# Matmuls of constants in TensorE's early gaps, and new planner constants, in a fused attention and MLP kernel

## The chip, the cores and the metric

The kernel runs on one core of one Trainium2 chip. A core has five engines with a queue each: TensorE (PE; its weight loads are shown apart as PEld), ScalarE (ACT), VectorE (DVE), GpSimd (POOL) and SyncE (SP), which here only issues DMAs. Each queue runs in its own order, and the engines wait for one another through semaphores. The metric is the device time of one execution in microseconds (us); the figure for a kernel is the median of several runs.

## The reference: what is computed

Inputs are q, k and v of shape (8, 8, 576, 64): eight batches, eight heads, 576 positions, 64 values. For each head two attentions are computed and added. In short, with `factor = 4`:

```python
q_d, k_d, v_d = (means over groups of 4 positions)      # 144 positions
out_d = softmax(scale * q_d @ k_d.T) @ v_d              # dense, small
out_up = repeat(out_d, 4)
mask = abs(i - j) < 4
out_local = softmax(where(mask, scale * q @ k.T, -1e9)) @ v
x = out_up + out_local                                  # to (4608, 512)
h = x @ w_in                                            # 512 -> 2048
out = (h * sigmoid(h)) @ w_out                          # 2048 -> 512
```

The output has 4608 rows of 512 float32. So there are 64 heads of attention, and behind them an MLP over 4608 tokens. The 512 values of a token come from all eight heads of its batch, so a token can enter the MLP only when all heads of its batch are done.

## The kernel before, in words

**The work.** Heads are handled in pairs (32) and in quads of two pairs (16); a batch is four pairs, or two quads. For each quad the tasks are, by their names in the code:

- `lqk`, `lv` (L403 on): SP loads q, k and v of a pair into staging tiles. For the first pairs some staging lies in tiles that are used only later (`gT`). `cq`, `ck`, `cw`: casts to bf16 on ACT, POOL or DVE.
- `TQ`, `TK` (`ph_T`): nine 128x128 transposes on PE into PSUM; `oq`, `ok` copy them out on ACT or DVE; `mq`, `mk` sum groups of four, on DVE or, for the first quads, on POOL.
- `S1`, `S2`: scores of the local band and of the small dense attention, followed by exponentials `e1`, `e2`, `e3` on ACT and `k`, the multiplication with the band's mask on DVE.
- `ZD` or `Z`: 56 small matmuls that sum the exponentials. For the first four quads ("direct") DVE forms a reciprocal split over three bf16 parts (`zs`, five operations) and PE spreads it over partitions (`RB`). For later quads DVE writes the reciprocal, SP sends it to memory (`scr`) and reads it back spread out (`Rb`).
- `VD`: 30 matmuls that downsample v for the direct quads; `cv` copies the result to `vd` in two operations. It needs the casts of both pairs' v.
- `PV`: probabilities times v of both attentions for a pair; `pa`, `pb` multiply with the reciprocals on DVE into `xo`; `ad` (L774) adds the two attentions on POOL and writes `xT`, the MLP's input.

The MLP takes 512 tokens at a time, nine such tiles. `g1` (L785 on) is four matmuls for one of 16 blocks of 128 hidden values, then a tanh on ACT (`th`) and a gate on DVE (`st`) into `gT`. `g2` is four matmuls of a quarter of one 128-token output block; behind the fourth quarter the result is copied to `osb` and stored. A `g1` of tile 0 needs the adds of the first four pairs (`ad0` to `ad3`).

**The order.** Nothing of the order is written out by hand. Before anything is emitted, a planner in the kernel (class `Prog`, and the loop at the kernel's end) plays the program through with a cost for each operation. At every step it takes, among the tasks that could start, one by its earliest start and by a priority: the dictionary `TUNE` holds one number for each kind of task, added to the start time. `seq` in `TUNE` is the order in which loads become ready for planning; `w0` to `w3` are the four quarters of `w_in`, `w4` to `w7` those of `w_out`, issued by POOL. The outcome is a fixed list for each engine, with semaphore waits. When the chip is late on one instruction, the rest of its engine's list waits behind it.

**PSUM.** There are eight banks: two `duo` pairs for attention, and `hps` and `ops`, which also serve attention until the first `g1` is planned. `best_bank` names a free bank.

The costs that the planner takes for PE are multiplied by 1.3 for what starts before 40 us of its own clock (L173).

Of the kernel before, what the change touches and what calls it, by code (L numbers as in the profile page):

```python
# [17 lines left out]


TUNE = {  # L20
    "tol": 0, "mode": -232, "lead": 52, "rep": 445, "g1": 743, "g2": 955, "TQ": -753, "TK": -555, "VD": -4771,
    "S1": -1491, "S2": -116, "ZD": -14158, "Z": 48, "RB": 750, "PV": -3123, "cw": 7042, "cv": 1981, "cq": -1820,
    "ck": 15017, "mask": -18259, "neg": 1254, "dm": 3746, "ones": 936, "Tq": 4085, "Tk": -7783, "mq": 1194,
    "mk": -571, "e1": -363, "e2": -2893, "e3": -162, "k": -4513, "rc": -10797, "zs": -8518, "rb": -4806,
    "pa": 6979, "pb": 21288, "th": 325, "st": -3659, "ob": 1342, "oq": 5641, "ok": 6128, "ad": 3736,
    "lqk": 14883, "lv": 9202, "lvq": 9231, "r": 13022, "b": 10108, "tq": -1796, "tk": 9538, "out": -3589,
    "age": 768, "alt": 538, "late": 900, "slack": 500, "slack1": 300, "direct": 4, "dma": 9, "cx": 6286,
    "c.dm": 29564, "c.pad": -7887, "c.vd": -1605, "band": 11289, "sel": 7263,
    "seq": ["lqk0", "lv0", "lqk1", "lqk2", "lv1", "lqk3", "lv2", "lv3", "w1", "lqk4", "w2", "w0", "w3", "lqk5",
            "lv4", "lqk8", "lqk7", "lqk6", "lv5", "w6", "w7", "lv6", "w4", "lqk9", "lv7", "w5"],  # L30
}


# [19 lines left out]
class Prog:  # L53
# [80 lines left out]
    def op(self, eng, fn, r=(), w=(), dma=None, cost=0, issue=450, tau=90, lock=False):  # L134
        op = Op(eng, fn)
        op.cost = cost
        op.pos = len(self.streams[eng])
        know = self.know[eng]
        deps = []
        for x in r:  # L140
            if x.psum:
                deps += [(o, False) for e, o in x.last.items() if e != eng]
            else:
                deps += [(o, True) for o in x.writers]
        for x in w:
            if x.psum:
                deps += [(o, False) for e, o in x.last.items() if e != eng]
            else:
                rd = x.readers + ([op] if x in r else [])
                if rd:  # L150
                    x.prev, x.readers, x.writers = rd + x.writers, [], []
                deps += [(o, dma is not None or eng != "PE") for o in x.prev]
                if dma is not None:
                    deps += [(o, True) for o in x.writers if o.dsem != dma]
        if eng == "POOL" and cost >= 400 and not dma and self.streams["POOL"] and not self.streams["POOL"][-1].dsem:

            deps.append((self.streams["POOL"][-1], True))
        deps = [(d, f) for d, f in deps if d is not op]
        t = self.free[eng]
        for d, f in deps:  # L160
            if d.eng != eng or d.dsem:
                t = max(t, d.end + self.LATENCY[d.eng])
        if dma:
            op.t0 = t
            t += issue if eng == "SP" else 650 if eng == "ACT" else 800
            self.free[eng] = max(t, self._dma(op, eng, t, cost, tau) if eng != "POOL" else t)
            if eng == "POOL":
                self._dma(op, eng, t, cost, tau)
        else:
            if lock or eng == "POOL":  # L170
                t = max(t, self.lock)
            op.t0 = t
            self.free[eng] = op.end = t + cost * (1.3 if eng == "PE" and t < 40000 else 1)  # L173
        if lock or (eng == "POOL" and not dma):
            self.lock = op.end
        op.deps = [d for d, f in deps]
        op.tag = self.tag
        deps.sort(key=lambda df: -(df[0].pos if not df[0].dsem else 1 << 30))
        for d, f in deps:
            self._dep(op, d, know, f)  # L180
        op.waits = [
            w for w in op.waits
            if not any(v is not w and v[2].K.get(w[0], -1) >= w[1] for v in op.waits)
        ]
        for x in r:
            if x.psum:
                x.last[eng] = op
            elif x not in w:
                x.readers.append(op)
        for x in w:  # L190
            if x.psum:
                x.last[eng] = op
            else:
                x.writers.append(op)
        op.K = dict(know)
        if dma:
            self.dcount[dma] = self.dcount.get(dma, 0) + 16
            op.dsem, op.dval = dma, self.dcount[dma]
            op.K[dma] = op.dval
        else:  # L200
            op.K[eng] = op.pos
        self.streams[eng].append(op)
        return op
# [36 lines left out]
def bass_hourglass_attn__then__act_silu_kernel(  # L240
# [9 lines left out]
    with kctx:  # L250
        E = kctx.enter_context
        P = Prog()
        res = {}

        def R(name, psum=False):
            if name not in res:
                res[name] = Res(name, psum)
            return res[name]

        def sb(name, shape, dt, n=1):  # L260
            ts = [E(nc.sbuf_tensor(f"{name}{i}", shape, dt)) for i in range(n)]
            return ts if n > 1 else ts[0]
# [6 lines left out]
        th = sb("th", [128, 512], F32, 2)  # L269
# [27 lines left out]
        id_bf = sb("id_bf", [128, 128], BF16)  # L297
        mask_bf = sb("mask_bf", [128, S_], BF16)
        onesZ = sb("onesZ", [128, 12, 32], BF16)
        neg = sb("neg", [128, 2], F32)  # L300
        band = sb("band", [128, 2, 10, 2], BF16)
        sel = gT[1][:, 11:16, :].rearrange("p a (y m) -> p (a y) m", m=128)
# [3 lines left out]
        duo = [E(nc.psum_tensor(f"duo{i}", [128, 2, 512], F32)) for i in range(2)]  # L306
# [3 lines left out]
        duo_r = [[R(f"{n}{x}", True) for x in y] for n, y in (("duo0", "ab"), ("duo1", "ab"), ("h", "01"), ("o", "01"))]  # L310

        direct, by_dma = tuple(range(TUNE["direct"])), tuple(range(TUNE["dma"], NQUAD))
# [105 lines left out]
        def order_T(s, x, eng):  # L418
            y, h = s % NQT, s % 2
            src = (qr if x == "q" else kr)[:, :, 64 * h:64 * h + 64].rearrange("p r g -> p g r")  # L420
            dst = (qT if x == "q" else kT)[y][:, :].rearrange("p (g r) -> p g r", r=9)
            r, w = [R(f"{x}r")], [R(f"{x}T{y}")]
            if eng == "DVE":
                P.op("DVE", lambda e: e.tensor_reduce(dst, src.unsqueeze(3), mybir.AxisListType.X, ALU.add),
                     r=r, w=w, cost=1165)
            else:
                copy(eng, dst, src, r, w, {"ACT": 1220})
# [43 lines left out]
        ng1, ng2 = [0], [0]  # L471
# [3 lines left out]
        def is_free(banks):  # L475
            return not any(pend.get(b.name) for b in banks)
# [14 lines left out]
        def best_bank():  # L491

            bs = [(d, x) for d in range(4 if ng1[0] == 0 else 2) for x in range(2) if is_free([duo_r[d][x]])]
            return min(bs, key=lambda b: (is_free([duo_r[b[0]][1 - b[1]]]), P.ready("PE", [], [duo_r[b[0]][b[1]]]), used[b[0]]),
                       default=None)
# [13 lines left out]
        done = set()  # L509
# [25 lines left out]
        mode = ["full"]  # L535
# [318 lines left out]
        seq = TUNE["seq"]  # L854
# [22 lines left out]
        for i in range(NQUAD):  # L877
# [10 lines left out]
            for s in (2 * i, 2 * i + 1):  # L888
                y, m, j = s % NQT, s % NP_, s % 2
                for x in "qk":  # L890
                    if i in by_dma:
                        task(("DVE", "ACT") if x == "q" else ("ACT", "DVE"), f"o{x}{s}",
                             [f"t{x}{i}", nm("S2", s - NQT), nm("mq", s - NQT), nm("mk", s - NQT)],
                             lambda e, s=s, x=x: order_T(s, x, e), [R(f"{x}r")], [R(f"{x}T{y}")])
# [78 lines left out]
        def choose(eng):  # L973

            c = [(s, t) for t in Q[eng][:LOOK[eng]] for s in [start(eng, t)] if s is not None]
            if eng != "PE":
# [10 lines left out]
                c.append((s + TUNE[k] + (TUNE["lead"] * lead * (1 if k == "g1" else -1)) + (TUNE["rep"] if last[0] == k else 0), s, k))  # L987
            return min(c, key=lambda x: x[0])[1:] if c else None

        LOOK = {"PE": 60, "ACT": 60, "DVE": 300, "POOL": 300, "SP": 70}  # L990
        last, log = [""], []
        const_id()
        while True:
            best = [(c[0], e, c[1]) for e in P.ENGS for c in [choose(e)] if c]
            if not best:
                break
            s, eng, t = min(best, key=lambda x: x[0])
            if isinstance(t, str):
                P.tag = last[0] = t
                n = ng1 if t == "g1" else ng2  # L1000
                (g1 if t == "g1" else g2)(*divmod(n[0], 16))
                log.append((s, t))
                continue
            for e in t[8]:
                Q[e] = [x for x in Q[e] if x is not t]
            if t[0] == f"ad{oldest[0]}":
                oldest[0] += 1
            for b in t[7]:
                pend[b.name] -= 1
            P.tag = t[0]  # L1010
            if eng == "PE":
                last[0] = t[0]
            t[2](eng)
            done.add(t[0])
            log.append((s, t[0]))
# [36 lines left out]
```

## Time and profile before

| | |
|---|---|
| median of 7 runs | 373.25 us (370.89 to 374.38) |
| profiled execution, its time | 373.78 us |
| profiled execution, its span from first to last instruction | 372.1 us |
| mean granted TensorE clock | 0.976 |
| PE busy | 346.1 us, 93% |
| DVE, ACT, POOL busy | 232.9, 218.3, 163.3 us |
| MLP matmuls, `g1` | 576, of which 544 into `hps`, 437 ns each |
| MLP matmuls, `g2` | 576, 381 ns each |
| moved by DMA | 66.13 MB, mean 178 GB/s |

The page cuts the span into 40 slices of 9.3 us. A digit of 9 is an engine busy for nine tenths of a slice or more; PEclk is the clock granted to TensorE in tenths of full speed. Matmul durations overlap, so 437 ns is not the spacing: four `g1` matmuls follow one another in 0.93 us at full clock. In a timeline, a bracket behind a line tells how long the engine was idle before it and what ended that. Time in which PE is idle, or slow, counts here; time in which another engine idles counts only through PE.

### The profile page before, as it was taken

Reading aid. Unit: us, or ns where it says so; the run is one execution under the profiler, and the core shown is the slowest. Engines: PE = TensorE matmul, PEld = TensorE weight load, DVE = VectorE, ACT = ScalarE, POOL = GpSimd, SP = SyncE. Lnnn points to the kernel's source line nnn. Section 1 sums busy time; section 2 is a strip of 40 time slices with the busy share of each in tenths; the row PEclk is TensorE's granted clock in tenths of the full one; section 3 lists DMA queues with packets and bytes.
Section 4 is the critical chain, followed back from the end, with each engine's and each line's share of the span. In section 5 each row is a group of like instructions: output and inputs, shape, how many; then the busy total and the mean of one; then the engine's idle time right before and its main releaser. Section 6 shows DMA issues by size and latency. Waiting matters only on the chain.

```text
span 372.1 us, 8434 instructions
## 1 busy us (share of the span) xinstructions
PE 346.1 (93%) x3498; PEld 213.5 (57%) x3498; DVE 232.9 (63%) x375; ACT 218.3 (59%) x362; POOL 163.3 (44%) x203
## 2 busy tenths in 40 slices
PE   1676899999979989999999999999999999999996
PEld 0565567566646655566556555556566555555542
DVE  4777478778578946795598469967765333333310
ACT  4967476587537753886588647766743343443321
POOL 7937665787288529643782286066113000000000
PEclk9978599999999999999999999999999999999999
DMA  7999979969999999999997899784144010001012
GB/s 235 322 359 345 185 218 261 193 184 254 245 241 256 189 284 242 242 237 258 249 243 182 187 190 174 201 179 101 35 116 106 28 56 28 30 28 56 30 56 85
DMA packets 85095, 66.13 MB, mean 178 GB/s; under 512 B 62785, under 2 KB 64833, under 8 KB 85057
## 3 DMA queue, kind: packets, MB, share of 16 engines
q1 hardware_dynamic: 80832, 59.31, 65.9%
q0 software_dynamic: 4224, 6.29, 7.3%
q8 instruction: 27, 0.44, 0.5%
q14 instruction: 12, 0.09, 0.1%
HBM read 53.67 MB, written 9.88 MB: 171 GB/s over the span
## 4 chain that ended last, share of the span: by engine, by line
PE 82%; DMA 7%; POOL 3%; DVE 3%; ACT 2%; SPq 1%; issue 1%; POOLq 0%; ACTq 0%
PE ops L541 35%; PE hps L541 34%; PE duo L541 11%; DMA scr<-rr 3%; DMA Rb<-scr 3%; PE duo L551 2%; POOL xT L774 2%; DMA qs<-in_q_dram 1%; POOL qb L382 1%; DVE xo L754 1%; DVE Pt L611 1%; ACT Pt L588 0%; SPq L443 0%; POOL w_out_bf L834 0%; DVE xo L757 0%
## 5 line engine op out<-in xcount | busy, mean ns | idle before, releaser
L541 PE MATMUL hps<-xT,w_in_sb 128*128 128x512 f32 x544 | 171.1, 437 | 4.5 <-DVE gT L797 2.9
L541 PE MATMUL ops<-w_out_bf,gT 128*128 128x512 bf16 x576 | 145.5, 381 | 0.0
L797 DVE SCALAR_TENSOR_TENSOR gT<-th,hps 128x512 bf16<-128x512 f32 x136 | 92.6, 683 | 81.1 <-ACT th L795 80.5
L795 ACT ACTIVATE th<-hps 128x512 f32<-128x512 f32 x136 | 81.5, 600 | 96.7 <-PE hps L541 96.0
L541 PEld LDWEIGHTS hps<-xT,w_in_sb 128*128 128x128 f32 x544 | 99.7, 190 | 33.2 <-DVE gT L797 3.9
L541 PEld LDWEIGHTS ops<-w_out_bf,gT 128*128 128x128 bf16 x576 | 46.6, 98 | 68.9 <-issue 29.0
L774 POOL TENSOR_TENSOR xT<-xo 128x576 fp32r<-128x576 f32 (+2 forms) x40 | 40.3, 1008 | 55.2 <-DVE xo L757 52.5
L611 DVE TENSOR_TENSOR Pt<-Pt,mask_bf 128x1152 bf16<-128x1152 bf16 x32 | 28.1, 884 | 6.6 <-ACT Pt L603 5.7
L378 ACT ACTIVATE osb<-ops 128x512 f32<-128x512 f32 x30 | 18.0, 599 | 22.1 <-PE ops L541 22.0
L588 ACT ACTIVATE Pt<-duo 128x912 bf16<-128x912 f32 x29 | 26.9, 929 | 6.1 <-PE duo L541 6.0
L754 DVE TENSOR_TENSOR xo<-duo,Rb 128x456 f32<-128x456 f32 x30 | 18.9, 629 | 15.1 <-DMA Rb<-scr 12.3
L382 POOL CAST qb<-qs 128x576 bf16<-128x576 f32 x24 | 18.3, 763 | 18.1 <-DMA qr<-qb 14.5
L575 DVE TENSOR_REDUCE qd<-qT 128x144 bf16<-128x576 bf16 x29 | 21.4, 746 | 6.7 <-ACT qT L378 3.5
L465 POOL TENSOR_TENSOR vd<-vq 112x384 bf16<-112x384 f32 (+1 forms) x24 | 24.5, 1021 | 2.2
L463 POOL TENSOR_TENSOR vq<-vq 112x768 f32<-112x768 f32 x12 | 22.0, 1833 | 4.3 <-DMA vq<-in_v_dram 2.9
L382 POOL CAST kb<-ks 128x576 bf16<-128x576 f32 x26 | 18.9, 726 | 11.1 <-DMA kr<-kb 4.7
L575 DVE TENSOR_REDUCE kd<-kT 128x144 bf16<-128x576 bf16 x29 | 21.3, 742 | 0.9 <-ACT kT L378 0.7
L382 POOL CAST vb<-vs 128x640 bf16<-128x640 f32 x10 | 7.6, 755 | 23.4 <-PE duo L541 22.8
L378 ACT ACTIVATE vb<-vs 128x640 bf16<-128x640 f32 x20 | 14.5, 733 | 3.2 <-PE duo L541 1.8
L541 PEld LDWEIGHTS duo<-qT,kT 64*128 64x128 bf16 x286 | 8.3, 97 | 12.7 <-issue 4.7
L378 ACT ACTIVATE kT<-kr 128x576 bf16<-128x576 bf16 x12 | 14.9, 1239 | 0.0
L541 PE MATMUL duo<-qT,kT 64*128 64x112 bf16 (+1 forms) x286 | 13.5, 218 | 1.2 <-DVE xo L754 0.8
(123 smaller groups left out, 330.8 us busy)
## 6 DMA issues: line engine op xcount, KB each, us to landing
vs<-in_v_dram SPq DMA_DIRECT2D x60, 160.0 KB, 5.3
out_dram<-osb SPq DMA_DIRECT2D x36, 256.0 KB, 2.4
Rb<-scr SPq DMA_DIRECT2D x24, 360.0 KB, 5.6
qs<-in_q_dram SPq DMA_DIRECT2D x29, 288.0 KB, 5.3
ks<-in_k_dram SPq DMA_DIRECT2D x29, 288.0 KB, 5.4
vq<-in_v_dram SPq DMA_DIRECT2D x24, 288.0 KB, 5.0
w_in_sb<-in_moe_w_in_dram POOLq DMA_DIRECT2D x4, 1024.0 KB, 12.4
w_out_bf<-in_moe_w_out_dram POOLq DMA_DIRECT2D x4, 512.0 KB, 7.2
```

Of the source, the lines that this page charges most:

```text
L378: fn = lambda e: e.activation(dst, src, AF.Copy, scale=1.0 if scale is None else scale)
L382: fn = lambda e: e.tensor_copy(dst, src)
L463: pool(lambda g: g.tensor_tensor(t, t, z[0:112], ALU.add), r=[R("vq"), R("vqz")], w=[R("vq")], cost=1900)
L465: pool(lambda g, a=a, n=n: g.tensor_tensor(vd[m][0:n, a, :, :, :].rearrange("p i h d -> p h i d"), x[0:n], y[0:n], ALU.add), r=[R("vq"), R ...
L541: return P.op("PE", lambda t: t.matmul(out_, lhsT, rhs, start=start, stop=stop, skip_group_check=True), r, w, cost=cost)
L575: P.op("DVE", lambda e: e.tensor_reduce(dst[j][:, 0:144], src[y][:, :].rearrange("p (g r) -> p g r", r=4), mybir.AxisListType.X, ALU.add), ...
L588: later("ACT", f"e1{p}", [(lambda e: e.activation(Pt[m][:, :, 0:456], D[:, :, 0:456], AF.Exp, scale=0.125), bk, [R(f"P{m}")], 930)], bk)
L611: P.op("DVE", lambda e: e.tensor_tensor(Pt[m][:, :, :], Pt[m][:, :, :], mask_bf[:, :].unsqueeze(1).to_broadcast([128, 2, S_]), ALU.mult), ...
L754: later("DVE", f"pa{p}", [(lambda e: e.tensor_tensor(xo[x][:, 0:456], D[:, 0, 0:456], Rb[u][:, 0:456], ALU.mult), [bk[0], R(f"Rb{u}")], [R ...
L774: P.op("POOL", lambda e, dst=dst, in0=in0, in1=in1: e.tensor_tensor(dst, in0, in1, ALU.add), r=[R(f"xo{x}")], w=xblk(kc, t, e_), cost=200 ...
L795: later("ACT", f"th{n}", [(lambda e: e.activation(th[tb][:, :], hp, AF.Tanh, scale=0.5), [hr], [R(f"th{tb}")], 597)], [hr], pre=[f"st{n - ...
L797: later("DVE", f"st{n}", [(lambda e: e.scalar_tensor_tensor(gT[j % 2][:, f, :], th[tb][:, :], 1.0, hp, ALU.add, ALU.mult), [hr, R(f"th{tb} ...
```

## The change

Three things change.

1. A new function `keep_on` in the planner's loop. When the next task is one of PE and would start at `s`, later than PE is free, it puts matmuls of the identity with 256 columns of the mask into a free bank. Nobody reads them; the next real matmul into the bank overwrites them. Their number is the gap less 200 ns (and a margin once the MLP has begun), times 0.6, over 110 ns each. None is put after 60 us of the planner's clock, before the mask is planned, or where no bank is free.
2. The planner's factor for early matmuls is 1.05 instead of 1.3.
3. Nearly all numbers of `TUNE` differ, `seq` among them, so the order on every engine differs, and the useful work doesn't.

```diff
-    "tol": 0, "mode": -232, "lead": 52, "rep": 445, "g1": 743, "g2": 955, "TQ": -753, "TK": -555, "VD": -4771,
+    "tol": 30, "mode": -232, "lead": 50, "rep": 315, "g1": 677, "g2": 955, "TQ": -672, "TK": -465, "VD": 151,
...
-    "c.dm": 29564, "c.pad": -7887, "c.vd": -1605, "band": 11289, "sel": 7263,
-    "seq": ["lqk0", "lv0", "lqk1", "lqk2", "lv1", "lqk3", "lv2", "lv3", "w1", "lqk4", "w2", "w0", "w3", "lqk5",
-            "lv4", "lqk8", "lqk7", "lqk6", "lv5", "w6", "w7", "lv6", "w4", "lqk9", "lv7", "w5"],
+    "cx": 9771, "c.dm": 33911, "c.pad": -15601, "c.vd": 2187, "band": 6941, "sel": 15975, "fill": 60,
+    "seq": ["lqk0", "lv0", "lqk1", "lv2", "lqk3", "lqk2", "lv1", "w0", "lv3", "w1", "lqk4", "w3", "lqk5",
+            "lv4", "w2", "lqk6", "w6", "lqk7", "lv5", "lqk8", "w5", "lv6", "w4", "lqk9", "w7", "lv7"],
...
-            self.free[eng] = op.end = t + cost * (1.3 if eng == "PE" and t < 40000 else 1)
+            self.free[eng] = op.end = t + cost * (1.05 if eng == "PE" and t < 40000 else 1)
...
+        def keep_on(s):
+
+            b = best_bank()
+            free = P.free["PE"]
+            if s > 60000 or "mask" not in done or b is None or P.ready("PE", [R("id"), R("mask")], [duo_r[b[0]][b[1]]]) > free:
+                return
+            for _ in range(int((s - free - 200 - (TUNE["slack"] if ng1[0] else 0)) * TUNE["fill"] / 11000)):
+                P.op("PE", lambda t: t.matmul(duo[b[0]][:, b[1], 0:256], id_bf[:, :], mask_bf[:, 0:256], start=True, stop=True,
+                                              skip_group_check=True), [R("id"), R("mask")], [duo_r[b[0]][b[1]]], cost=110)
...
+            if eng == "PE":
+                keep_on(s)
```

On PE the outcome is 67 such matmuls, L997 in the new listing. In the new order they stand in these groups:

```
9 transposes q, 11 fillers, 9 transposes k, 4 fillers, S1, 5 fillers, S1, S2, S2, 3 fillers,
9 transposes q, 4 fillers, 9 transposes k, 4 fillers, ZD, S1, S1, S2, 2 fillers, S2, RB, RB,
ZD, VD, 6 fillers, PV, PV, RB, RB, 5 fillers, VD, 6 fillers, PV, PV,
9 transposes q, 5 fillers, 9 transposes k, 4 fillers, S1, S1, S2, 2 fillers, S2, 4 fillers, first g1 ...
```

In the order before, `VD` of the first quad stands ahead of the first `S1`, and there are no fillers. On POOL the list before is: add 0, add 1, two weight loads, two means (two operations each), add 2, a cast, add 3. The new list is: a v cast, add 0, add 1, add 2, one weight load, add 3, a mean. SP's first six loads are the same.

## The prediction

> **What bounds the kernel now.** I read the page's busy table first, then the slices, the table of windows and the timelines. The busy table and two slice rows:
>
> ```profile
> PE 346.1 (93%) x3498; PEld 213.5 (57%) x3498; DVE 232.9 (63%) x375; ACT 218.3 (59%) x362; POOL 163.3 (44%) x203
> ...
> PE   1676899999979989999999999999999999999996
> ...
> PEclk9978599999999999999999999999999999999999
> ```
>
> TensorE works for 346.1 of 372.1 us, so 26.0 us are idle. The PE timeline places them: 7.7 before the first transpose, 10.2 in named gaps up to 42 us, 4.6 between 75 and 140 us (0.64, 1.36, 0.75, 0.28 and 1.58), 3.2 behind the last matmul. From 145 to 369 us there is none: there the kernel is its matmuls. So time is won only by earlier useful work in the first 45 us, by a faster clock there, or from the few later waits. The windows show the clock (columns: PE, PEld, DVE, ACT, POOL busy, clock, DMA share, GB/s):
>
> ```profile
> 18.20:21.60 3.40, 2.12 (x78) 1.87 (x80) 3.33 (x7) 2.24 (x5) 2.87 (x5) 0.67 1.14 381
> 21.60:25.00 3.40, 2.10 (x38) 1.52 (x34) 2.50 (x6) 3.35 (x8) 0.50 (x1) 0.82 1.21 349
> 31.90:35.30 3.40, 2.11 (x46) 1.55 (x40) 3.37 (x7) 2.37 (x5) 3.31 (x5) 1.00 1.08 381
> 38.70:42.10 3.40, 1.86 (x5) 1.32 (x5) 0.14 (x1) 0.91 (x3) 3.12 (x5) 0.50 1.27 221
> 42.10:45.50 3.40, 3.40 (x63) 2.35 (x61) 2.03 (x4) 1.75 (x4) 1.61 (x2) 0.50 1.10 178
> ```
>
> The first MLP matmuls run at half clock until about 46.7 us (0.83 in 45.5 to 49). Why they start where they do is in the PE and POOL timelines:
>
> ```profile
> 37.34 1.62 PE L541 MATMUL hps<-xT,w_in_sb 128*128 128x512 f32 x3
> 40.49 2.50 PE L541 MATMUL hps<-xT,w_in_sb 128*128 128x512 f32 x5 [1.54 <-POOL xT L774]
> 42.80 1.91 PE L541 MATMUL ops<-xT,w_in_sb 128*128 128x512 f32 x4
> ```
> ```profile
> 32.69 1.53 POOL L834 DMA_DIRECT2D w_out_bf<-in_moe_w_out_dram  x2
> 34.23 0.69 POOL L570 TENSOR_TENSOR vq<-qT 128x288 f32<-128x288 bf16 x1
> ...
> 36.74 1.21 POOL L774 TENSOR_TENSOR xT<-xo 128x576 fp32r<-128x576 f32 x1
> 38.09 1.00 POOL L382 CAST qb<-qs 128x576 bf16<-128x576 f32 x1
> 39.24 1.21 POOL L774 TENSOR_TENSOR xT<-xo 128x576 fp32r<-128x576 f32 x1
> ```
>
> Tile 0 needs all four adds; the fourth ends at 40.45, behind weight issues, means and a cast on GpSimd.
>
> [...] The trace agrees on half rate (four matmuls of 512 columns take 1.9 us there, 0.93 later), but 0.67 in 18.2 to 21.6 means that it fell near 19.4, and the 3.4 us before that held one gap of 1.5 (17.9 to 19.4)[...]
>
> **The change, part by part.**
>
> *Fillers.* The new order holds 67, in 15 groups of 2 to 11, all ahead of the first MLP matmul but the last group of two. 67 x 0.109 = 7.3 us warm, 14.3 cold: I put most of this into idle time (18 us lie there). They read `mask_bf`, finished on GpSimd at 4.2 us, well before the first group. Exposed is what overruns: the first 11 begin at 8.84 and last 2.35 us cold, to 11.2; the K transposes behind them could start at 10.7 (their cast now directly follows the qT copies), so 0.45 us is lost, yet they start no later than before (11.27). Later groups of four or five stand before waits of 0.5 us and more; the four ahead of the first MLP matmul cost 0.44 outright. Bounds of what is exposed: 0.4, and 3 if my gaps are not there. The changed factor (1.3 to 1.05) enters the planner's costs alone and emits nothing.
>
> *The new constants* move tasks on all engines. Walking the new order with the durations of the rows:
> - V's downsampling (30 matmuls, 2.1 us cold) leaves the place before the first scores. K transposes end 12.3, ACT's kT copy 13.05, first exp 13.7 (before 14.97). VectorE gives this back: it makes a mean (0.75) before its kT copy and takes a cast (0.75), so mask 0 ends at 19.55 (19.38), the first reciprocal chain at 22.75 (22.41), the second at 27.85 (28.06). To here: nothing.
> - The downsampling now stands behind the second sums: 0.96 us warm, and two copies of 0.49 on ACT; the first PV ends 28.3, its products 29.1. The second downsampling waits for a V cast that ends 30.65; its copies end 32.8, PV3 33.5, the last product 34.75 (35.96).
> - GpSimd now does adds 2 and 3 with one weight issue (0.77) between: 33.9 to 35.1, 35.9 to 37.1. That is 3.3 us before 40.45.
> - Now late next: quad 2. Its casts end 34.1 (ACT) and 35.5 (DVE), transposes 36.1, copies 37.4; GpSimd's mean waits behind add 3 and ends 38.7; S2 to 39.1, four fillers to 39.55. There the first eight MLP matmuls start and run through.
> - Same work, both orders: before, 16 MLP matmuls with one sums group and one transpose end at 47.62. After: 39.55 + 16 x 0.234 + 0.57 + 0.50 = 44.4, if warm. Gain 3.2. If half clock persists from 39.55 to about 46, some 3 us of it go.
>
> *Loads.* GpSimd issues two 1 MB weight loads after two selects, near 7.3 to 9.1 us (before one at 10.2). Q/K of pairs 2 and 3 end a first 3.0 MB in both orders; at 340 GB/s shared with 2 MB, the last lands between 12.5 (weights last) and 17.7 (weights first). I take 16; its cast comes at 17.1 on GpSimd, so 0 to 0.6 us exposed. SP's own first six issues are unchanged. Behind a waiting cast on DVE stand mask and reciprocal chain, so lateness would pass on one to one.
>
> *Later waits.* VectorE's product with `Rb` waits for the DMA, and the gate operations behind it hold the banks:
>
> ```profile
> 102.14 0.63 DVE L754 TENSOR_TENSOR xo<-duo,Rb 128x456 f32<-128x456 f32 x1 [3.68 <-DMA Rb<-scr]
> ...
> 138.54 0.63 DVE L754 TENSOR_TENSOR xo<-duo,Rb 128x456 f32<-128x456 f32 x1 [3.42 <-DMA Rb<-scr]
> ```
>
> PE paid 1.36 and 1.58. Between sums and PV stood 9.9 us of PE work at the second; the new order puts 11.3 there: minus 1.4. At the first it is 9.5 and 9.6, but `scr` is now issued ahead of one V load, worth 0 to 0.9. The 0.64 wait at 75 us ends if two S groups no longer abut a transpose (an MLP group now stands between). Against these some new wait must be expected: at the second place SP now puts the scr of the next quad before this quad's Rb, which comes when both sums are done, 5.8 us apart. I take minus 1.0 for all later waits, bounds minus 3 and plus 3.
>
> *The rest* is unchanged: per kind the same number of useful matmuls (576, 576 and so on), 337 against 332 group boundaries behind the first MLP one, at 0 to 0.2 us each (bounds minus 1, plus 0.5; I take 0), the final 68 matmuls the same.
>
> Sum: 372.1 - 3.2 - 1.0 = 367.9 span. The profiled execution took 373.78, so 1.68 lies around the span: 369.6. It stood 0.53 above the median of 373.25: 369.1.
>
> **Rivals.** 0.5% (371.4 and 375.1) is about what this kernel's spread can tell from no change.
> - *The fillers don't hold the clock.* The fall after a window 56% busy speaks for it: the new timeline still has holes of 0.7 to 2 us (23.4 to 25.4 has no filler at all)[...]. Against it, the last 7 us before 39.55 are about 70% busy. Cost 3: 372.1.
> - *Gains come, then later waits give them back.* PE ahead by 3 us meets the same `scr`/`Rb` transfers (5.4 and 5.6 us each). For it: DMA share over 1 through 180 us. Against: loads were rarely waited for. 369.1 + 3 = 372 to 373.
> - *Slower: SP's order at the second Rb.* This Rb now waits for the next quad's sums (5.8 us after its own), reciprocal (1.2), then 0.4 + 5.6 for the transfer: it lands about 13.4 us after its sums, PE needs it at 16. Slack 2.6. If SP's transposes ahead (1.3 to 3.6 us each) hold it up, each further us is a stalled PE. It ends slower than before once it comes 8 to 9 us later than this: 375.5 to 377.
> - *The change does nothing in sum:* fillers late as often as they help: 373.
>
> **How the numbers follow.** Forecast 0.55, its own range 366.5 to 371.3; clock not held 0.17 (half of it within 0.5%, a third still faster); gains given back 0.13; slower 0.13; nothing 0.02. Faster: 0.55 + 0.08 = 0.63; slower 0.13 + 0.01 = 0.14; same 0.23. The range 366 to 374.2 takes in the bounds of loads and waits and leaves out most of the slower case and little below.
>
> **What would show it.** Right: PEclk 9 or 10 tenths between 37 and 47 us; MLP start at 39 to 40 us without a gap behind; fourth xT add ending near 37; no Rb wait over 1 us of PE at 130 to 140. Wrong: MLP start after 41; clock 0.5 behind it; mask or casts on DVE waiting for qs or ks before 20 us; PE idle over 3 us between 50 and 300.

## The result and the profile after

The changed kernel takes 370.13 us, the median of 26 runs, against 373.1 us (63 runs) for the kernel before in the same measurement: a ratio of 0.9929 with a 95% interval of 0.9913 to 0.9945. It is faster by 3.0 us. Two later sessions (below) gave 0.9937 and 0.9903. Medians are of all runs; the ratios, and the half clock below, leave out the slow ones, which are those over 1.5% above the fastest run of their kernel. The profiled execution took 370.65 us, with a span of 368.9 us against 372.1.

The page of the changed kernel, its busy table and two of the slice rows:

```profile
PE 349.0 (95%) x3565; PEld 215.2 (58%) x3565; DVE 232.7 (63%) x377; ACT 216.7 (59%) x362; POOL 158.8 (43%) x199
...
PE   1877999999799999999999999999999999999996
...
PEclk9999999999989999999999999999999999999999
```

There are 67 matmuls more, and PE is busy for 2.9 us more in a span that is 3.2 us shorter. The clock row has lost the dip of slices 3 to 5 (before: 7, 8, 5). The windows of the same kernel show this closer (columns: PE, PEld, DVE, ACT, POOL busy, granted clock, DMA share, GB/s):

```profile
18.20:21.60 3.40, 2.96 (x99) 1.93 (x96) 3.29 (x7) 2.88 (x5) 2.53 (x4) 1.00 1.19 340
21.60:25.00 3.40, 1.30 (x76) 1.18 (x76) 2.82 (x5) 2.10 (x5) 0.76 (x2) 1.00 1.14 382
...
31.90:35.30 3.40, 2.85 (x69) 2.26 (x63) 1.69 (x5) 2.23 (x4) 0.54 (x1) 1.00 1.10 351
...
38.70:42.10 3.40, 3.33 (x32) 2.41 (x32) 1.62 (x2) 3.18 (x8) 3.06 (x5) 1.00 1.01 191
42.10:45.50 3.40, 3.40 (x76) 2.56 (x75) 3.17 (x8) 2.46 (x6) 2.00 (x4) 1.00 0.93 159
```

From 38.7 to 45.5, where the kernel before had 0.50, the clock is full. In the PE timeline of the changed kernel (start, duration, operation, and in brackets the idle time before it) the first MLP matmuls look like this:

```profile
27.95 0.47 PE L541 MATMUL hps<-osb,gT 128*128 128x72 bf16 x9
29.86 0.21 PE L541 MATMUL hps<-osb,gT 128*128 128x72 bf16 x1 [1.45 <-issue]
...
40.37 2.06 PE L541 MATMUL hps<-xT,w_in_sb 128*128 128x512 f32 x8
...
42.93 1.19 PE L541 MATMUL ops<-xT,w_in_sb 128*128 128x512 f32 x4
...
44.45 1.17 PE L541 MATMUL ops<-xT,w_in_sb 128*128 128x512 f32 x4
45.46 1.08 PE L541 MATMUL hps<-xT,w_in_sb 128*128 128x512 f32 x4
```

Eight MLP matmuls take 2.06 us in one piece; before, they were cut into three and five by the wait for the fourth add, and the five took 2.50 us at a granted clock of 0.50. The work that was done at 47.62 before (16 MLP matmuls, one sums group, one transpose group) is done at 45.46. Both are the start of the operation that follows it; in the kernel before this is:

```profile
47.62 1.17 PE L541 MATMUL hps<-xT,w_in_sb 128*128 128x512 f32 x4
```

The adds on GpSimd, from its timeline in the changed kernel:

```profile
34.76 1.21 POOL L774 TENSOR_TENSOR xT<-xo 128x576 fp32r<-128x576 f32 x1 [3.90 <-DVE xo L757]
35.91 0.79 POOL L834 DMA_DIRECT2D w_out_bf<-in_moe_w_out_dram  x1
36.72 1.22 POOL L774 TENSOR_TENSOR xT<-xo 128x576 fp32r<-128x576 f32 x1
38.32 0.67 POOL L570 TENSOR_TENSOR vq<-kT 128x288 f32<-128x288 bf16 x1 [0.37 <-ACT kT L378]
```

The fourth add ends at 37.9 (40.45 before). It no longer sets the MLP's start: PE reaches the first MLP matmul behind quad 2's scores and four fillers.

After 46 us one wait of PE over 0.25 us is left, where there were five before. Two of the five, from the PE timeline of the kernel before:

```profile
103.76 1.20 PE L541 MATMUL hps<-xT,w_in_sb 128*128 128x512 f32 x4 [1.36 <-DVE gT L797]
...
140.16 1.21 PE L541 MATMUL hps<-xT,w_in_sb 128*128 128x512 f32 x4 [1.58 <-DVE gT L797]
```

The one that is left, from the PE timeline of the changed kernel, and below it the windows of that stretch:

```profile
101.00 1.93 PE L541 MATMUL hps<-xT,w_in_sb 128*128 128x512 f32 x4 [1.85 <-DVE gT L797]
```
```profile
97.80:101.20 3.40, 1.55 (x8) 0.55 (x7) 1.82 (x4) 0.60 (x1) 0.77 (x1) 1.00 0.61 210
101.20:104.60 3.40, 3.40 (x9) 1.77 (x9) 1.91 (x4) 0.60 (x1) 3.04 (x4) 0.50 0.98 231
```

The waits of 0.64, 0.75, 0.28 and 1.58 are gone. The one at the first `Rb` grew from 1.36 to 1.85, and in this execution a window of half clock followed it, which by my estimate costs another 1.7 us (half of its 3.4).

### The profile page after: what moved, and what is told of

It is laid out like the page before. It is cut to its first block, busy times and chain, and to the rows that moved or that the text cites. A ratio compares the mean times of both kernels' runs of the same rounds, so it can differ in the third digit from the quotient of the medians.

```text
span 368.9 us, 8560 instructions
## 1 busy us (share of the span) xinstructions
PE 349.0 (95%) x3565; PEld 215.2 (58%) x3565; DVE 232.7 (63%) x377; ACT 216.7 (59%) x362; POOL 158.8 (43%) x199
## 4 chain that ended last, share of the span: by engine, by line
PE 77%; DMA 8%; POOL 4%; DVE 4%; ACT 3%; SPq 2%; issue 1%; POOLq 0%; DVEq 0%; ACTq 0%
PE ops L541 33%; PE hps L541 30%; PE duo L541 10%; DMA Rb<-scr 4%; DMA kr<-kb 2%; PE duo L551 2%; DMA scr<-rr 2%; PE duo L997 1%; DMA qs<-in_q_dram 1%; POOL vd L465 1%; POOL vq L463 1%; DVE Pt L611 1%; SPq L649 1%; POOL xT L774 1%; SPq L408 1%
## 5 line engine op out<-in xcount | busy, mean ns | idle before, releaser
L378 ACT ACTIVATE osb<-ops 128x512 f32<-128x512 f32 x33 | 19.8, 599 | 22.1 <-PE ops L541 22.0
L382 POOL CAST qb<-qs 128x576 bf16<-128x576 f32 x26 | 19.4, 744 | 24.7 <-DMA qr<-qb 13.9
L611 DVE TENSOR_TENSOR Pt<-Pt,mask_bf 128x1152 bf16<-128x1152 bf16 x32 | 26.2, 821 | 5.0 <-ACT Pt L603 3.5
L575 DVE TENSOR_REDUCE qd<-qT 128x144 bf16<-128x576 bf16 x31 | 22.9, 747 | 3.0 <-ACT qT L378 1.8
L382 POOL CAST kb<-ks 128x576 bf16<-128x576 f32 x25 | 16.7, 669 | 10.4 <-PE duo L551 4.5
L382 POOL CAST vb<-vs 128x640 bf16<-128x640 f32 x12 | 9.4, 785 | 20.6 <-PE duo L541 19.6
L605 ACT ACTIVATE Pd<-duo 128x432 bf16<-128x432 f32 x30 | 16.1, 540 | 0.0
L378 ACT ACTIVATE vb<-vs 128x640 bf16<-128x640 f32 x18 | 13.1, 733 | 2.1 <-DMA vs<-in_v_dram 1.0
L541 PE MATMUL duo<-Pt,vb 128*64 128x120 bf16 (+1 forms) x310 | 13.6, 217 | 0.3 <-ACT Rb L378 0.2
```

Source lines behind the costliest of these rows:

```text
L378: fn = lambda e: e.activation(dst, src, AF.Copy, scale=1.0 if scale is None else scale)
L382: fn = lambda e: e.tensor_copy(dst, src)
L541: return P.op("PE", lambda t: t.matmul(out_, lhsT, rhs, start=start, stop=stop, skip_group_check=True), r, w, cost=cost)
L575: P.op("DVE", lambda e: e.tensor_reduce(dst[j][:, 0:144], src[y][:, :].rearrange("p (g r) -> p g r", r=4), mybir.AxisListType.X, ALU.add), ...
L611: P.op("DVE", lambda e: e.tensor_tensor(Pt[m][:, :, :], Pt[m][:, :, :], mask_bf[:, :].unsqueeze(1).to_broadcast([128, 2, S_]), ALU.mult), ...
```

## The experiments

All were run with the kernel before on the same chip, in three sessions (first: nofill, fill_only, fill_double, gates_first; second: changed_again, rb_ahead, early_fillers, late_fillers; third: the last three). "Half clock" is an estimate of the mean time at half rate over the runs that the ratios use, from each run's mean granted clock c and span s: taking all lost clock as half rate, it is 2(1 - c)s. The kernel before had 14.8 to 16.1 us of it, the changed kernel 1.8 to 2.5. Except in fill_only the order of all useful work is that of the changed kernel, unless a move is named. None leaves out useful work. A profile is of one execution, and executions differ early: the first transposes start between 7.5 and 9.1 us, and all later marks shift with them.

| run | what | us (before beside it) | ratio, 95% | half clock |
|---|---|---|---|---|
| e1 nofill | new order, no fillers | 371.91 (373.25) | 0.9961 [0.9939, 0.9983] | 7.5 |
| e10 nofill again | the same | 372.12 (372.83) | 0.9981 [0.9957, 1.0006] | 6.1 |
| e2 fill_only | order before, 40 fillers | 372.21 (373.25) | 0.9961 [0.9939, 0.9983] | 14.2 |
| e3 fill_double | new order, 131 fillers | 371.83 (373.25) | 0.994 [0.991, 0.9969] | 2.9 |
| e4 gates_first | two products behind two gates | 371.24 (373.25) | 0.9948 [0.9925, 0.9972] | 4.4 |
| e5 changed again | as changed | 370.21 (372.84) | 0.9937 [0.9915, 0.9959] | 1.8 |
| e11 changed third | as changed | 369.03 (372.83) | 0.9903 [0.9876, 0.9931] | 2.0 |
| e6 rb_ahead | an `Rb` ahead of two loads | 372.96 (372.84) | 1.0009 [0.9992, 1.0026] | 6.8 |
| e7 early_fillers | first 31 of the 67 | 369.35 (372.84) | 0.9911 [0.9879, 0.9942] | 9.7 |
| e8 late_fillers | last 36 of the 67 | 368.5 (372.84) | 0.9886 [0.9862, 0.9909] | 1.6 |
| e9 late again | the same | 368.52 (372.83) | 0.99 [0.9864, 0.9936] | 0.2 |

### The order alone (e1_nofill, e10_nofill_again)

```diff
-    ... "sel": 15975, "fill": 60,
+    ... "sel": 15975, "fill": 0,
```

> The changed kernel without its 67 fillers; every other instruction and the order on all five engines are those of the changed kernel. If the fillers work by holding the clock: half clock returns in several 3.4 us windows before 47 us, the first 8 MLP matmuls take up to 4 us instead of 2.0, and 2 to 4 us of the 2.6 us gain are lost: ratio to the kernel before 0.998 to 1.003. If the new order alone makes the gain: ratio 0.991 to 0.995, with the MLP starting up to 0.5 us earlier than 40.4 because the four fillers ahead of it are gone.

> The same kernel as e1_nofill (new order, no fillers), a second time. Theory 'order and fillers are worth about the same, 1.2 to 1.4 us each': ratio 0.994 to 0.998, half-clock time 6 to 10 us, 1 to 2 us above the changed kernel in the same call and 2 to 3.5 above e9_late_again. Rival 'the new order alone carries the gain': ratio below 0.993, within 0.5 us of the changed kernel.

Without fillers the new order is 0.7 to 1.3 us faster than before; e1's ratio lies between its two forecasts, and the interval of e10 takes in no change. Against the changed kernel on the same chip it is 3.1 us slower (372.12 to 369.03), more than the 1 to 2 that I expected: on this chip fillers are worth more than order. The size is less sure: e1's 0.9961 against the changed kernel's first 0.9929 would make it 1.2 us, in different sessions. Their place is seen in the PE timelines. First the new order without fillers (e10):

```profile
41.12 3.75 PE L541 MATMUL hps<-xT,w_in_sb 128*128 128x512 f32 x8 [0.38 <-ACT Pt L588]
...
48.65 1.08 PE L541 MATMUL hps<-xT,w_in_sb 128*128 128x512 f32 x4
...
103.25 1.21 PE L541 MATMUL hps<-xT,w_in_sb 128*128 128x512 f32 x4 [0.91 <-DVE gT L797]
...
112.65 1.04 PE L541 MATMUL ops<-w_out_bf,gT 128*128 128x512 bf16 x4 [0.57 <-ACT osb L378]
```

Then the changed kernel on that chip (e11):

```profile
40.14 2.08 PE L541 MATMUL hps<-xT,w_in_sb 128*128 128x512 f32 x8
...
45.25 1.08 PE L541 MATMUL hps<-xT,w_in_sb 128*128 128x512 f32 x4
...
100.75 1.19 PE L541 MATMUL hps<-xT,w_in_sb 128*128 128x512 f32 x4 [1.80 <-DVE gT L797]
```

The mark at which before stood at 47.62 is reached at 48.65 without fillers and at 45.25 with them: 3.4 us earlier, of which 1.0 is there at the first MLP matmul (0.2 of it already at the first transposes, 8.13 and 7.90), 1.7 comes in the first eight (3.75 to 2.08; e10's granted clock is 0.65 from 38.7 to 42.1 and 0.50 from there to 45.5, e11's is 1.00), and 0.7 in what follows. At 101 us a part is given back: the wait is 1.80 with fillers and 0.91 without. The spans differ by 2.8 (369.9 and 367.1). So the order alone does not bring the MLP forward at all: it reaches the mark 1.0 us later than before (e1 too, at 48.61), and it gains because the later waits of PE shrink from 4.6 to 1.7 us.

### The fillers in the order before (e2_fill_only)

```diff
-    "c.dm": 29564, ... "sel": 7263,
+    "c.dm": 29564, ... "sel": 7263, "fill": 60,
...
+            if eng == "PE":
+                keep_on(s)          # as in the change, but cost=0: no task moves
```

> The kernel before, its order kept on all engines, with 40 fillers put into its own planned gaps (15 behind the first transposes, 15 ahead of the first MLP matmul). If the clock is what counts: clock 1.0 from 37 to 47 us, which was half, worth about 4 us, less up to 1 us by which the 15 fillers ahead of the MLP overrun: ratio 0.990 to 0.994. If the order is what counts: ratio 0.998 to 1.004.

Forty fillers in the idle stretches of the order before gain about 1.0 us by the medians, between the two forecasts, and half clock stays at 14.2 us per run. In its profile three gaps of PE stay bare, without a filler (1.88 us at 19.8, 1.21 at 25.8, 1.72 at 34.7), and the granted clock is 0.58 from 18.4 to 21.8, 0.50 from there to 28.6, 0.91 to 32.0, and 0.50 from 36.0 to 39.4. The 15 fillers ahead of the MLP run from 37.8, and the first eight MLP matmuls behind them, from 40.15, take 2.27 us. Fillers gain 1.0 us here and 3.1 in the new order; but these are 40 and 67 fillers, in different sessions, so that the order makes the difference is not shown.

### Twice as many fillers (e3_fill_double)

```diff
-    ... "fill": 60,
+    ... "fill": 115,
...
-  [duo_r[b[0]][b[1]]], cost=110)
+  [duo_r[b[0]][b[1]]], cost=0)
```

> The changed kernel with nearly twice the fillers in the same gaps, order of all useful work unchanged. The clock is already full, so nothing is to be gained there; groups that fill a planned gap to its end overrun it where the true gap is shorter, 0.2 to 0.5 us each at some five places, and the group ahead of the MLP costs 0.4 us more: ratio 0.993 to 0.998. If 60% of the gaps was too thin to hold the clock in most runs: ratio 0.988 to 0.992.

Half clock 2.9 us and a ratio of 0.994, as forecast for gaps filled too far: no more than with 67. In its profile (span 371.2):

```profile
9.07 1.14 PE L551 MATMUL duo<-id_bf,qb 128*128 128x128 bf16 x9 [9.07 <-ACT qb L378]
...
44.47 2.09 PE L541 MATMUL hps<-xT,w_in_sb 128*128 128x512 f32 x8
```

The first MLP matmul starts at 44.47 us, in the changed kernel at 40.37. Of these 4.1 us, 1.4 are the first transposes, which start at 9.07 instead of 7.64, behind ScalarE's cast in both (the bracket above). The other 2.7 come behind them, where 131 fillers stand instead of 67. Here fillers that outlasted their gap delayed the work they were to serve.

### The wait at 101 us (e4_gates_first, e6_rb_ahead)

Two ways to take that wait away. In e4 the products `pa8`, `pb8` (and with them the next pair's) stand behind two gates on VectorE; in e6 SP sends the quad's first `Rb` (`b4`) ahead of two V loads. Lists as planned, D: VectorE, S: SP:

```diff
-  ... D:pa8 D:pb8 ... D:st27 D:pa9 ... D:pb9 ... D:st28
+  ... D:st27 ... D:st28 D:pa8 D:pb8 ... D:pa9 D:pb9
```
```diff
-  ... S:lv14 ... S:lvq6 ... S:b4
+  ... S:b4 S:lv14 S:lvq6
```

> The changed kernel with one edit: on VectorE the first two products with Rb (pair 8, at 99.4 us) stand behind two more gate operations of the MLP instead of ahead of them. If the wait of 1.85 us of PE at 101 us comes only from that place in VectorE's queue, it goes, and with it the half-clock window behind it (about 1.7 us): ratio 0.984 to 0.989. If the late Rb then holds up PE at the next place (the banks of pair 10): ratio 0.991 to 0.994.

> The changed kernel with one edit on SP: the first Rb transfer is issued ahead of one v load and one vq load (3 instructions moved, all else in place). In the changed kernel it is issued at 90.3 us and lands at 99.3, 9.0 us later, where 5.6 is the median. If the two loads in the rings ahead of it make it late: it lands near 96, VectorE's wait of 3.3 us ends, PE's wait of 1.85 us at 101 goes and nothing follows: span minus 1.5 to 3, ratio 0.984 to 0.990. If the transfer is late for the traffic in general: it lands at 98 or later, ratio 0.991 to 0.995.

The wait did go, from 1.7 to 1.85 down to nothing in e4 and to 0.69 in e6. In e6 the `Rb` goes out at 89.37, 1.2 us earlier than in e5, and its product starts at 95.99 without a wait, 3.6 us earlier than in e5: at least 2.4 us of its lateness came from the two loads ahead of it. Both kernels were no better for it: e6 is slower than the changed kernel on the same chip by 2.7 us, more than either theory allowed. The PE timeline of e6, in its fastest execution (371.53 us):

```profile
99.83 1.21 PE L604 MATMUL hps<-xT,w_in_sb 128*128 128x512 f32 x4 [0.69 <-DVE gT L860]
...
108.13 0.71 PE L604 MATMUL duo<-qT,kT 64*128 64x120 bf16 x8 [0.55 <-DVE xo L817]
109.61 0.56 PE L604 MATMUL duo<-qT,kT 64*128 64x120 bf16 x2 [0.77 <-DVE xo L817]
...
111.21 1.32 PE L604 MATMUL ops<-w_out_bf,gT 128*128 128x512 bf16 x4 [0.70 <-ACT osb L441]
```

and its windows:

```profile
108.00:111.40 3.40, 1.56 (x19) 0.89 (x20) 1.89 (x5) 1.58 (x4) 2.60 (x4) 1.00 1.17 307
111.40:114.80 3.40, 3.40 (x15) 2.30 (x14) 1.47 (x2) 1.79 (x4) 0.90 (x2) 0.56 1.20 180
```

The next pair's products now come late instead: SP sends their `scr` behind the two loads, at 93.36 (92.33 in e5), and their `Rb` at 100.95 (99.77), and VectorE waits 3.24 us for it, to 107.4. PE stands for 0.55 + 0.77 + 0.70 = 2.0 us within one stretch, and the granted clock is 0.56 in the window behind it, worth 1.5 by my estimate (0.44 of 3.4). In e4 PE waits at the same place, once for 2.07, with a clock of 0.60 in the window behind. There it is not a transfer that makes VectorE late: the profile puts its waits of 1.89 and 1.62 us down to GpSimd. The wait of PE in e4:

```profile
109.57 0.56 PE L604 MATMUL duo<-qT,kT 64*128 64x120 bf16 x2 [2.07 <-DVE xo L817]
```

With marks on PE, whose useful work has the same order in all of them, the exchange is plain. Start of the products near 104 us, and of those near 134: changed kernel 104.14 and 133.49 (e5), 103.68 and 133.26 (e11), 105.56 and 134.51 in its first profile, with the window of half clock; e6 102.78 and 136.33; e4 102.39 and 135.53. Against e5 and e11 each arrives 1 to 2 us earlier and leaves 2 to 3 later.

### Which fillers count (e7_early_fillers, e8_late_fillers, e9_late_again)

```diff
-            if s > 60000 or "mask" not in done or ...
+            if s > 19000 or "mask" not in done or ...               # e7
+            if s > 60000 or s < 19000 or "mask" not in done or ...  # e8, e9
```

> The changed kernel with only its first 31 fillers (six groups, up to the first sums at 18.9 us), order unchanged. If the clock at the start of the MLP is what counts, these do not hold it there: half clock in part of 36 to 47 us, ratio 0.995 to 0.998, near that of the kernel without fillers (0.996). If the early chain counts, most of the fillers' gain stays: 0.992 to 0.994.

> The changed kernel with only its last 36 fillers (nine groups, from 20 us on), order unchanged. If the clock at the start of the MLP is what counts, these alone hold it: clock 1.0 from 37 to 47 us, ratio 0.991 to 0.994. If the early chain counts: 0.995 to 0.998.

> The same kernel as e8_late_fillers (the changed kernel's order, and of its fillers only the last 36), a second time, beside the changed kernel and the one without fillers on the same chip. Theory 'the late fillers are enough, and the early 31 cost something': ratio to before 0.987 to 0.991, 1 us or more below the changed kernel, mean half-clock time under 4 us. Rival 'the 0.005 between it and the changed kernel was chance': ratio 0.991 to 0.995, within 0.5 us of the changed kernel.

> The changed kernel itself once more, to stand on the same chip as the three that follow. Ratio to the kernel before 0.991 to 0.995 if its first comparison holds.

> The changed kernel once more, as the measure for e9_late_again and e10_nofill_again: ratio 0.991 to 0.995, half-clock time 1 to 4 us. All theories expect the same of it.

With the late 36 alone the clock is full at the MLP's start (half clock 1.6 and 0.2 us; e9's windows read 1.00 from 38.7 to 49.0); with the early 31 alone the first eight MLP matmuls take 3.75 us again (from 40.16; 2.08 in e11) and half clock is 9.7. Yet e7 is not slower than the changed kernel: 369.35 against 370.21, intervals overlapping. In its profile:

```profile
40.16 3.75 PE L604 MATMUL hps<-xT,w_in_sb 128*128 128x512 f32 x8 [0.66 <-ACT Pt L651]
```

So each theory did as well as it had forecast, or better, in the run that was made for it (0.9911 for the early chain, 0.9886 and 0.99 for the clock): either half of the fillers brings the whole gain, and the gains don't add up (e7 and e8 are seven and six runs of one session, e9 seven of another). The early half gains though its first eight MLP matmuls take 3.75 us. Against e1, whose first transposes start at the same time (7.55 and 7.56 us), e7 is 1.0 us ahead at the first MLP matmul, 2.0 at the products near 134 and 2.7 in the span. How delays are made up, in one profile of each (e7 is of another session):

| mark on PE, us | e11 changed | e9 late | e7 early | e10 none |
|---|---|---|---|---|
| first products of quad 2 | 57.25 | 58.12 | 59.12 | 60.65 |
| products before the wait | 94.06 | 94.93 | 96.19 | 97.45 |
| the wait | 1.80 | 0.69 | 0.62 | 0.91 |
| products after it | 103.68 | 103.44 | 104.63 | 106.20 |
| products near 134 us | 133.26 | 133.01 | 134.09 | 136.17 |
| span | 367.1 | 366.8 | 367.6 | 369.9 |

e9 is 0.87 us behind the changed kernel until 95 us and 0.24 ahead of it at 103; e7 makes up 1.2 of 2.1. The wait differs as much between executions of one kernel: in e8, the kernel of e9, it is 1.48, as PE arrives 0.2 us earlier (94.73) and the product with `Rb` starts 0.6 later (99.47 against 98.88). In the PE timeline of e9 it is this line, to be set beside the one at 100.75 of e11:

```profile
100.50 1.19 PE L604 MATMUL hps<-xT,w_in_sb 128*128 128x512 f32 x4 [0.69 <-DVE gT L860]
```

What PE waits for is set elsewhere: SP's queue, from its timelines, first of e11, then of e9:

```profile
90.00 1.32 SPq L649 DMA_DIRECT2D Rb<-scr  x2
```
```profile
90.19 1.32 SPq L712 DMA_DIRECT2D Rb<-scr  x2
```

`Rb` is issued at the same time in both, though PE was 0.9 us apart. An early PE only waits longer. Without any fillers `Rb` goes out at 93.16, and there the delay passes through.

Are the late fillers alone better than all 67? In the second session by 1.7 us (368.5 to 370.21), in the third by 0.5 (368.52 to 369.03), within its intervals. The forecast for e9, 1 us or more below the changed kernel, was missed. The early ones aren't needed beside the late ones, nor, by e7, the late beside the early; that the early ones cost something stays open. Both runs of the late ones are the fastest kernel here, about 4.3 us below the kernel before.

## Why the prediction was right, and where it was off

I predicted 369.1 us; it is 370.13, and the later sessions gave 370.21 and 369.03. In span the forecast was a gain of 4.2; the profile has 3.2, and those of e5 and e11 have 4.2 and 5.0. The parts of the sum:

- **Start gain, 3.2.** Measured 2.16 (47.62 to 45.46), 1.84 in e5 and 2.37 in e11. Up to the first products the walk holds (they end at 29.09, forecast 29.1). The term that failed is "the second downsampling waits for a V cast that ends 30.65". It ended at 31.5, since ScalarE makes it behind the copy of the spread reciprocal, and that copy starts only at 30.11: PE's `RB` group stood for 1.45 us in the middle (the line at 29.86 above). The last product therefore ended at 35.55 instead of 34.75, VectorE's cast behind it at 36.2 instead of 35.5, and the MLP began at 40.37 instead of 39.55. The other 0.24 us are the 16 MLP matmuls and two groups, 5.09 us instead of 4.85. In e11 the stop isn't there, but the clock was at 0.60 from 25.0 to 28.4 and the copy starts at 29.87 all the same.
- **Fillers and loads.** The first 11 fillers run from 8.57, 0.21 us apart, though the granted clock reads 1.00 there, and the K transposes behind them start 2.35 us later, at 10.92 (forecast 11.2, before 11.27). The six from 26.05 follow one another in 0.11 us (forecast 0.109). DMA moved 332 to 348 GB/s in the windows from 8.0 to 18.2 (my estimate took 340). GpSimd's cast of the K load starts at 16.81 (forecast 17.1); PE waits 0.64 for it, and the first sums start at 18.87 all the same, before 19.48.
- **The clock at the MLP's start.** Right: full from 38.7 on. The rival "the fillers don't hold the clock" had a price of 3 and a time of 372.1. e10 has that price, 3.4 at the mark, and 372.12 us, without any fillers. But e7 shows that the clock there does not settle the time: the first eight MLP matmuls took 3.75 us, and the kernel 369.35.
- **What the new order brings.** My walk gave the start gain to new order and fillers together. e10 and e1 show the order alone 1.0 us later at the mark than before; all of the gain there is the fillers', and what the order gains comes later.
- **Later waits, minus 1.0.** That the sum came out is luck: two errors cancel. The second `Rb` wait (1.58) ended, as argued, by more PE work between sums and products; the 0.64 ended too. I had not counted the 0.75 and 0.28, which also went. But the first, for which I allowed a gain of 0 to 0.9, lost 0.49, and the window of half clock behind it took 1.7: 0.64 + 0.75 + 0.28 + 1.58 - 0.49 - 1.7 = 1.06. I saw that `scr` goes out ahead of one V load, and passed over that `Rb` still stands behind two. With the start gain of 2.16 this makes the measured 3.2. e5 and e11 have no such window of half clock, hence their 4.2 and 5.0.
- **Rivals.** "Gains come, then later waits give them back" happened in part: 0.9 of 3.4 us at 101 us between e10 and e11. "Slower by SP's order at the second `Rb`" did not: VectorE waits 2.35 us for it at 138.7, and PE is busy for 9.87 of the 10 us from 130 to 140.
- **Signs.** Full clock from 37 to 47, and no `Rb` wait over 1 us of PE at 130 to 140: as said. The fourth add ended at 37.9 instead of 37.1, and the MLP start at 40.37 missed "39 to 40" but had no gap behind it. None of the signs of a wrong prediction was seen.

Three causes stay open: what stops PE inside the `RB` group (below), why the early and the late fillers gain as much alone as together, and whether the early ones cost something beside the late.

## What to carry to other kernels

Idle time ahead of a dense stretch of matmuls can cost twice, as at 101 us in the changed kernel's first profile: once as a wait (1.85 us) and once as half clock behind it (0.50 for 3.4 us, estimated at 1.7). Fillers sized to less than the gap paid here; either half of them paid as much as all, and 131 no more than 67, so try fewer first, and judge by the time and not by the clock. Look for the next wait that is set by something other than PE, for it gives part of any earlier gain back. And where a wait on a transfer is removed, ask where lateness comes out next: here PE stood 8 us later, for longer (2.0 us in e6, 2.07 in e4), and the clock behind it was 0.56 and 0.60.

## What the runs showed of the hardware

- How much idle time of PE makes the granted clock fall is not shown; that these fillers would hold it was an estimate of mine. In the changed kernel a window with 1.55 us of work in 3.4, one wait of 1.85 within it, was followed by one at 0.50 (97.8 to 104.6, above). In e6 it was 1.56 (108.0 to 111.4) and 0.56 behind it. In the kernel before, 1.80 us of work in 16.0 to 19.4 (that is 53%, not the 56 of the prediction) was followed by 0.50 from 19.4 to 22.8. But one wait is no certain sign: 1.80 us at the same place in e11 and 1.73 in e5 were followed by 1.00 (101.2 to 104.6). And with 1.30 busy in 21.6 to 25.0 the clock stayed at 1.00 to 28.4 in the changed kernel, while in e11 the same 1.30 had 0.90 and was followed by 0.60. No run shows what makes the difference.
- PE stops for 0.27 to 1.45 us with nothing to wait for ("issue") near its 350th matmul, inside the `RB` group, in before (0.63), the changed kernel (1.45), e4 (0.27), e5 (1.32) and e6 (1.44), and not in e1, e2, e3, e7, e8, e9, e10 and e11. Loads fill the DMA engines then, but no less in runs without the stop (share 1.22 from 28.4 to 31.8 in the changed kernel and in e9 alike). The cause is open.
- Time at half clock alone does not tell how fast a kernel is: e7 has 9.7 us of it per run and takes 369.35 us, e5 has 1.8 and takes 370.21, e10 has 6.1 and takes 372.12. Part of the delay is made up where PE would wait anyway: between 94 and 104 us e7 makes up 1.2 of its 2.1 us on e11, with a wait of 0.62 against 1.80.
